# A gated-attention kernel with a fused maxout layer: the second sequence's z fetched and transposed one step earlier, and a shorter lead time for one diagonal group

## The chip, the cores and the metric

The kernel runs on one core of one Trainium2 chip. A core has a matrix engine (TensorE, PE in the profile, with its weight loads as PEld), a vector engine (VectorE, DVE), a scalar engine (ScalarE, ACT), a general engine (GpSimd, POOL) and a queueing engine (SyncE, SP). They run side by side, each in its own program order, and wait for each other by semaphores. PSUM is the memory that TensorE writes; 16 DMA engines move data between memories. The metric is the device time of one execution in microseconds (us), as the median of several runs.

## The reference

Eight sequences of 3072 rows. Each goes through an attention with squared, rectified scores, is gated by u, and the result goes through a two-branch maxout layer:

```python
scale = 1.0 / S                                          # S = 3072, D = 256, d_qk = 64
scores = scale * np.matmul(z, z.transpose(0, 2, 1))
attn = np.maximum(scores, 0.0) ** 2
x = u * np.matmul(attn, v)                               # x: 24576 x 256
h1 = x @ w1                                              # d_ff = 1024
h2 = x @ w2
out = np.maximum(h1, h2) @ w_out
```

The kernel takes max(h1, h2) as max(x (w1 - w2), 0) + h2, so that the second branch folds into one matrix W2o = w2 @ w_out.

## The kernel before, in words

**Steps.** A sequence has 24 blocks of 128 rows; a step (b, s) makes the output of four of them, so there are 6 steps for each of 8 sequences, 48 in all, numbered through from 0. In step (b, s), TensorE sums 24 blocks into two PSUM tiles, `xacc0` and `xacc1` (256 columns in two halves; one buffer each, so a step's first xacc matmul waits until the step before has been read out). DVE then multiplies by u (the tile `xT`, lines 295 to 306). Three steps later (LAG = 3) the maxout part of that step runs: matmuls into `d_ps`, evicted as `g_sb` by ACT or DVE, then matmuls into `o_ps`, evicted as `o_sb` and written out. From step 4 on, all xacc, d and o matmuls are cut into half-height (64-row) ones.

**Scores.** A pair tile (n, k0) is the two score blocks k0 and k0 + 1 of step n against its four column blocks: two matmuls into `s_ps`, then ReLU on ACT (`r_sb`, line 233) and a square on DVE (`a_sb`, line 236). The score matrix is symmetric, so a pair to the right of the diagonal is also turned by a DMA transpose on SyncE's queue (`aT`) and serves a later step; in the first sequence the first four steps compute everything up to column group 3 directly. A diagonal tile (n, None) is made by `scores_diag` (line 249): four score matmuls into two buffers, one ReLU on ACT, one on DVE, four squares on DVE into `aD`, and three turns on SyncE.

**PSUM buffers.** `s_ps`, `d_ps`, `o_ps` and `w2o_ps` share three buffers (`mm_psum`, line 71) in turn.

**The order written out by hand.** The list `work` holds TensorE's work besides the scores, with nominal lengths in ns. Every item names the tiles that it reads and a latency, and a tile's due time is the item's nominal start minus that latency (line 650). Latencies: LAT_OWN for a tile read directly, LAT_TURNED for a turned one, LAT_DIAG for a diagonal (line 536, used in `put_block`, line 549). `lay` (line 678) then goes through the tiles from the last due to the first and puts each group at the last allowed spot that is not after its due time and far enough ahead of the group behind it. In the later steps a group is one tile; in the first steps it is three (WIN = 3), and in steps 0 to 2 the allowed spots are one nominal group of 2592 ns apart. The three first groups are put down by hand at the head of the kernel (`ahead`, `squared` and `third`, lines 786 to 814); among these, `third` scores the tiles (0,8) and (0,10).

**Transfers.** `plan` (line 711) gives each load and turn a nominal time, as a step and us into it; they are issued when the order of work passes that time (lines 815 to 823). Loads go out from GpSimd's queue, each behind a `gate`: a one-column copy of the newest score or g tile (line 97), which holds the load back until that tile exists. z of a sequence is loaded by `load_z` (line 103: one DMA that casts from fp32 to bf16, and two small memsets) and transposed into `zT` by `make_zT` (line 136: two DMA transposes on SyncE's queue). The times for the second sequence's z are `z_at` and `zT_at` in line 742. w_out is loaded at step 2 + 9 us and first read by `fold_w2o` in step 3 (line 187).

**Where the second sequence comes in.** The steps of the first sequence are 0 to 5. The first group that needs the second sequence's zT is the diagonal tile (6, None), which `lay` puts into step 4, behind 16 of that step's 24 blocks.

Of the kernel before, what the change touches and what calls it, by code (L numbers as in the profile page):

```python
# [11 lines left out]
def kernel(  # L12
# [32 lines left out]
    G = 4  # L45
# [487 lines left out]


    work = []
    LAT_OWN, LAT_TURNED, LAT_DIAG = 3500, 9000, 12000

    def put(ns, shares, fn, reads=()):
        work.append((ns, shares, fn, reads))
# [9 lines left out]
    def put_block(st, k):  # L549
        row = NG * st.b + st.s  # L550
        if k // G in st.early:
            reads = [((NG * st.b + k // G, k0), LAT_TURNED) for k0 in (G * st.s, G * st.s + 2)]
            put(216, False, lambda: st.add_early(k), reads)
        elif k // G == st.s and st.diag:
            put(216, False, lambda: st.add_diag(k % G), [((row, None), LAT_DIAG)])
        else:
            put(216, False, lambda: st.add_own(k), [((row, k - k % 2), LAT_OWN)])

# [19 lines left out]
    for n, st in enumerate(steps):  # L578
# [4 lines left out]
        if st.halves:  # L583


            blocks = [G * i + j for i in st.early for j in range(G)]
            blocks += [k for k0 in own for k in (k0, k0 + 1)]
            if st.diag:
                blocks += [G * st.s + j for j in range(G)]
            put_three_d(n - LAG)  # L590
            within = dict(zip((4, 10), put_d_halves(n - LAG, 6)))
            for i, k in enumerate(blocks):
                within.get(i, lambda: None)()
                put_block(st, k)
            put_all_o(n - LAG)
            within = {}
            if n == len(steps) - 1:
                within = dict(zip((14, 20), put_d_halves(n - LAG + 1, 6)))
                within[4] = lambda: put_three_d(n - LAG + 1)
            for i in range(NSB):  # L600
                within.get(i, lambda: None)()
                put(216, False, lambda st=st, i=i: st.other_way(i))
            continue
# [107 lines left out]
    def plan(b, s, us, is_load, fn):  # L711
        transfers.append((start_of[b, s] + us * 1000, len(transfers), is_load, fn))

    def plan_load(b, s, us, fn):
        plan(b, s, us, True, fn)

    def fetch_u(b, s):
        seqs[b].u_sb[s] = load_u(b, s)

    def turn_u(b, s):  # L720
        seqs[b].uT[s] = make_uT(seqs[b].u_sb[s])

    def fetch_z(b):
        seqs[b].z_sb = load_z(b, [NSB])
        seqs[b].v = new_v()

    def turn_z(b):
        seqs[b].zT = make_zT(seqs[b].z_sb)

    def fetch_v(b, i):  # L730
        load_v(b, seqs[b].v, i * G, G)

    for n, st in enumerate(steps):
        b, s = st.b, st.s
        if n + 1 < len(steps):
            nx = steps[n + 1]
            plan_load(b, s, 5 if st.halves else 2, lambda nx=nx: fetch_u(nx.b, nx.s))
        plan(b, s, 1, False, lambda b=b, s=s: turn_u(b, s))
        if s == 0 and b + 1 < B:
            c = b + 1  # L740
            if b == 0:
                z_at, zT_at = (3, 5), (4, 4)
                v_at = [(4, 8), (4, 14), (5, 1), (5, 6), (5, 11), (5, 15)]
            else:
                z_at, zT_at = (0, 7), (3, 3)
                v_at = [(s, 14) for s in range(NG)]
            plan_load(b, *z_at, lambda c=c: fetch_z(c))
            plan(b, *zT_at, False, lambda c=c: turn_z(c))
            for i, at in enumerate(v_at):
                plan_load(b, *at, lambda c=c, i=i: fetch_v(c, i))  # L750
# [103 lines left out]
```

## Time and profile before

| | |
|---|---|
| median of 3 runs | 977.18 us (976.05 to 978.23) |
| the profiled execution's own time | 974.66 us |
| its span, first to last instruction | 972.9 us |
| mean granted TensorE clock | 0.996 of full speed |
| DVE, ACT, POOL busy | 40%, 50%, 8% |
| DMA transposes and stores (queue q1), share of the 16 DMA engines' span | 66.0% |
| DMA loads with a cast (queue q0) | 23.3% |

The page gives busy times by engine and groups of instructions. `L77` is the line of a helper that records all matmuls, so groups are told apart by their tiles: `xacc<-a_sb,v_sb` adds a block whose scores are read directly, `xacc<-aT,v_sb` one that was turned, `xacc<-aD,v_sb` a diagonal one, `s_ps<-zT` are scores. `64*128` is a half-height matmul, two of which run side by side. In a timeline row stand the start in us from the start of the span, the length, the engine, line and operation, the tiles written and read, the count, and in brackets the idle time ahead of it with what ended it. Lengths of neighbouring matmuls overlap, so a rate is read from start to start. SPq is SyncE's queue: its lengths are those of issuing, not of the transfer. A row of the windows view has the window, its length, then for PE, PEld, DVE, ACT and POOL the busy time and the count, then the granted clock, the DMA share and GB/s.

### The profile page before, as it was taken

The numbers are of one execution on the slowest core, as the hardware profiler recorded it, in microseconds if no ns is written. First come the engines' busy times: TensorE is split into PE (matmuls) and PEld (weight loads), VectorE is DVE, ScalarE is ACT, GpSimd is POOL, SyncE is SP. The second block draws the span as 40 slices with busy tenths as digits, with TensorE's granted clock in tenths as the row PEclk, the third lists the DMA queues.
The fourth block names the chain that finished last, engine by engine and source line by source line (L and its number), as shares of the span: only waits on it lengthen the run. The fifth ranks groups of instructions, "written<-read, shape, count | busy, mean of one in ns | idle before, by whom it ended". The sixth has DMA issues, their size and how long they took to land.

```text
span 972.9 us, 24379 instructions
## 1 busy us (share of the span) xinstructions
PE 956.9 (98%) x10446; PEld 590.5 (61%) x10446; DVE 391.5 (40%) x648; ACT 485.9 (50%) x533; POOL 78.9 (8%) x228
## 2 busy tenths in 40 slices
PE   8996999999999999999999999999999999999998
PEld 3353655676667666666666666666666666666666
DVE  5662344334532454325433344333444333442211
ACT  6863445445553555445554454544555545554323
POOL 2110110000000001000010001000000000000000
PEclk9998999999999999999999999999999999999999
DMA  8997999989999899997998989978899889875411
GB/s 138 152 155 141 161 157 185 156 134 174 111 178 172 129 196 131 158 184 132 168 168 141 170 147 147 194 132 153 144 155 190 152 138 168 153 139 112 102 42 66
DMA packets 378557, 144.07 MB, mean 148 GB/s; under 512 B 356945, under 2 KB 358609, under 8 KB 378449
## 3 DMA queue, kind: packets, MB, share of 16 engines
q1 hardware_dynamic: 361888, 112.78, 66.0%
q0 software_dynamic: 16560, 29.74, 23.3%
q8 instruction: 81, 1.33, 0.6%
q14 instruction: 28, 0.22, 0.1%
HBM read 59.77 MB, written 25.17 MB: 87 GB/s over the span
## 4 chain that ended last, share of the span: by engine, by line
PE 96%; DMA 2%; DVE 1%; ACT 1%; issue 0%; SPq 0%; POOL 0%; DVEq 0%; POOLq 0%
PE xacc L77 51%; PE o_ps L77 22%; PE d_ps L77 16%; PE s_ps L77 7%; DMA v_sb<-in_v_dram 1%; DMA zT<-z_sb 1%; ACT r_sb L233 0%; DMA o_sb<-in_z_dram 0%; DVE g_sb L513 0%; PE tpz L149 0%; DVE a_sb L236 0%; PE w2o_ps L77 0%; DVE r_sb L231 0%; ACT r_sb L261 0%; ACT zT L150 0%
## 5 line engine op out<-in xcount | busy, mean ns | idle before, releaser
L77 PEld LDWEIGHTS <-v_sb 64*128 64x128 bf16 (+1 forms) x4416 | 255.5, 94 | 232.9 <-issue 8.3
L233 ACT ACTIVATE r_sb<-s_ps 128x1024 bf16<-128x1024 f32 x258 | 260.7, 1024 | 161.9 <-PE s_ps L77 159.1
L236 DVE TENSOR_TENSOR a_sb<-r_sb 128x1024 bf16<-128x1024 bf16 x260 | 179.4, 691 | 398.2 <-ACT r_sb L233 395.1
L77 PE MATMUL xacc<-a_sb,v_sb 64*128 64x512 bf16 (+1 forms) x1888 | 254.0, 377 | 1.2 <-DMA v_sb<-in_v_dram 1.0
L77 PE MATMUL xacc<-aT,v_sb 64*128 64x512 bf16 x1824 | 228.8, 376 | 0.0
L77 PE MATMUL o_ps<-w_out_sb,g_sb 64*128 64x256 bf16 (+1 forms) x3008 | 202.0, 269 | 0.4 <-ACT g_sb L513 0.2
L77 PE MATMUL d_ps<-xT,w_sb 64*128 64x512 bf16 (+1 forms) x1520 | 191.1, 376 | 0.2 <-ACT g_sb L513 0.2
L513 ACT ACTIVATE g_sb<-d_ps 128x1024 bf16<-128x1024 f32 x127 | 124.8, 1021 | 107.9 <-PE d_ps L77 105.2
L77 PEld LDWEIGHTS <-g_sb 64*128 64x128 bf16 (+1 forms) x3008 | 166.6, 94 | 11.8 <-issue 1.0
L77 PEld LDWEIGHTS <-w_sb 64*128 64x128 bf16 (+1 forms) x1520 | 85.5, 94 | 77.9 <-issue 1.3
L527 ACT COPY o_sb<-o_ps 128x512 f32<-128x512 f32 x92 | 53.8, 585 | 150.8 <-PE o_ps L77 150.8
L77 PE MATMUL s_ps<-zT 64*128 64x512 bf16 (+3 forms) x696 | 117.5, 357 | 9.1 <-DMA zT<-z_sb 7.9
L77 PE MATMUL xacc<-aD,v_sb 64*128 64x512 bf16 x704 | 92.2, 378 | 0.0
L513 DVE TENSOR_SCALAR g_sb<-d_ps 128x1024 bf16<-128x1024 f32 x61 | 74.7, 1225 | 39.9 <-PE d_ps L77 31.2
L77 PE MATMUL o_ps<-W2o_sb,xT 64*128 64x256 bf16 (+1 forms) x752 | 76.0, 269 | 0.0
L263 DVE TENSOR_SCALAR r_sb<-s_ps 128x384 bf16<-128x384 f32 x44 | 24.5, 558 | 112.3 <-PE s_ps L77 112.3
L77 PEld LDWEIGHTS <-zT 64*128 64x128 bf16 x696 | 37.3, 94 | 50.3 <-issue 9.3
L299 DVE SCALAR_TENSOR_TENSOR xT<-xacc,uT 128x512 bf16<-128x512 f32 x96 | 61.9, 683 | 14.5 <-PE xacc L77 14.5
L261 ACT ACTIVATE r_sb<-s_ps 128x896 bf16<-128x896 f32 x44 | 40.3, 917 | 49.8 <-PE s_ps L77 49.1
L98 POOL COPY gate_sb<-a_sb 128x1 bf16<-128x1 bf16 x75 | 14.4, 192 | 582.5 <-DVE a_sb L236 404.4
L77 PEld LDWEIGHTS <-xT 64*128 64x128 bf16 (+1 forms) x752 | 42.2, 94 | 0.4
L101 POOL DMA_DIRECT2D u_sb<-in_u_dram x48 | 25.5, 531 | 18.3 <-issue 17.6
(40 smaller groups left out, 127.8 us busy)
## 6 DMA issues: line engine op xcount, KB each, us to landing
out_dram<-o_sb SPq DMA_DIRECT2D x47, 512.0 KB, 3.4
v_sb<-in_v_dram POOLq DMA_DIRECT2D x48, 256.0 KB, 5.4
u_sb<-in_u_dram POOLq DMA_DIRECT2D x48, 256.0 KB, 5.2
aT<-a_sb SPq DMA_TRANSPOSE x228, 4.9
z_sb<-in_z_dram POOLq DMA_DIRECT2D x7, 384.0 KB, 8.8
aD<-aD SPq DMA_TRANSPOSE x132, 3.7
w_sb<-in_moe_w_dram POOLq DMA_DIRECT2D x2, 512.0 KB, 7.7
uT<-u_sb SPq DMA_TRANSPOSE x48, 3.8
```

The source lines that it names most:

```text
L77: return pin(nc.tensor.matmul(*args, **kw))
L98: pin(nc.gpsimd.tensor_copy(gate_sb, tile_ap))
L101: pin(nc.gpsimd.dma_start(**kw))
L233: keep(nc.scalar.activation(r_sb, s_ps, AF.Relu))
L236: keep(nc.vector.tensor_mul(a_sb, r_sb, r_sb))
L261: nc.scalar.activation(r_sb, s_ps[:, 0:7, :], AF.Relu)
L263: nc.vector.tensor_single_scalar(out=r2_sb, in_=s2_ps[:, 2:5, :], scalar=0.0, op=ALU.max)
L299: nc.vector.scalar_tensor_tensor(out=xT[:, dc, :].rearrange("p (t q) -> p t q", q=P), in0=xacc[dc].rearrange("p (t q) -> p t q", q=P), sca ...
L513: nc.any.tensor_single_scalar(out=g_sb, in_=d_ps, scalar=0.0, op=ALU.max)
L527: nc.any.tensor_copy(o_sb[:, ds(t, 2), :], o_ps[:, :, :D])
```

## The change

Two edits. The diagonal tiles of the first sequence (there are two of them: steps 4 and 5) get a latency of their own, 9500 instead of 12000, so their due time is 2.5 nominal us later. The second sequence's z is loaded at step 2 + 6 us instead of step 3 + 5 us, and transposed at step 3 + 8 us instead of step 4 + 4 us.

```diff
-    LAT_OWN, LAT_TURNED, LAT_DIAG = 3500, 9000, 12000
+    LAT_OWN, LAT_TURNED, LAT_DIAG_0, LAT_DIAG = 3500, 9000, 9500, 12000
...
-            put(216, False, lambda: st.add_diag(k % G), [((row, None), LAT_DIAG)])
+            put(216, False, lambda: st.add_diag(k % G), [((row, None), LAT_DIAG if st.b else LAT_DIAG_0)])
...
             if b == 0:
-                z_at, zT_at = (3, 5), (4, 4)
+                z_at, zT_at = (2, 6), (3, 8)
                 v_at = [(4, 8), (4, 14), (5, 1), (5, 6), (5, 11), (5, 15)]
```

## The prediction

> **What bounds the kernel now.** I read the page's busy times first, then the list of waits on TensorE, then the timeline around the longest of them.
>
> ```profile
> PE 956.9 (98%) x10446; PEld 590.5 (61%) x10446; DVE 391.5 (40%) x648; ACT 485.9 (50%) x533; POOL 78.9 (8%) x228
> ...
> PE s_ps L77 <- DMA zT<-z_sb: 7.9, 1, 7.9
> ...
> PE xacc L77 <- DMA v_sb<-in_v_dram: 1.0, 1, 1.0
> ```
>
> TensorE is busy for 98% of the span, so only what makes it wait, or run slowly, can pay. One wait is far longer than the rest: once, a score matmul waits 7.9 us for the transpose of a z. The timeline of TensorE shows where, with two groups ahead of it that ran undisturbed (start, length, tiles, count, and in brackets the idle time before it):
>
> ```profile
> 78.95 1.03 PE L77 MATMUL xacc<-aT,v_sb 64*128 64x512 bf16 x8
> 79.82 0.38 PE L77 MATMUL s_ps<-zT 64*128 64x512 bf16 x2
> ...
> 82.46 1.46 PE L77 MATMUL xacc<-aT,v_sb 64*128 64x512 bf16 x12
> 91.80 0.71 PE L77 MATMUL s_ps<-zT 64*128 64x512 bf16 x4 [7.88 <-DMA zT<-z_sb]
> 92.31 1.91 PE L77 MATMUL xacc<-a_sb,v_sb 64*128 64x512 bf16 x8
> 94.02 1.54 PE L77 MATMUL xacc<-aD,v_sb 64*128 64x512 bf16 x8
> 95.40 0.38 PE L77 MATMUL s_ps<-zT 64*128 64x512 bf16 x2
> ...
> 84.00:96.00 12.00, 4.20 (x30) 1.91 (x32) 1.64 (x6) 1.16 (x3) 1.24 (x3) 0.72 0.81 126
> ```
>
> The waiting group is the four score matmuls of the second sequence's first diagonal. After it TensorE is slow as well: eight half-height xacc matmuls take 0.87 us from 78.95 to 79.82, but 1.71 and 1.38 us from 92.31 and 94.02. The row of the 12 us window gives the reason: its granted clock (the third number from the end) is 0.72 of full speed.
>
> **The z transfers.** SyncE's queue and the landing times of the two transposes:
>
> ```profile
> 83.35 3.96 SPq L92 DMA_TRANSPOSE zT<-z_sb  x2
> ...
> DMA to landing us min/median/max: 6.0/6.5/7.0
> ...
> 62.61 0.53 POOL L101 DMA_DIRECT2D z_sb<-in_z_dram  x1 [0.26 <-issue]
> ...
> 83.04 1.02 ACT L513 ACTIVATE g_sb<-d_ps 128x1024 bf16<-128x1024 f32 x1
> ```
>
> They are issued at 83.35, just as TensorE comes to need them, and the second lands some 7 us later. The change puts the z load one step earlier on GpSimd's queue (ahead of w_out and the next u) and the transposes into step 3 on SyncE's queue, behind the turn of tile (3,16) and ahead of those of (3,18) to (3,22). That place on SyncE comes at about 62 to 66 us, so they land near 72, some 12 us before their use. The gain here is 7.88 us of idle time, plus the clock: 1.71 + 1.38 - 2 x 0.87 = 1.35 for the xacc matmuls, and half of the 0.51 us (91.80 to 92.31) of the four scores, 0.25: 1.6 together. In the sum: **-9.5**. Behind the wait something new can show: the diagonal needs two score buffers, and one belongs to a d_ps whose ACT eviction ended at 84.06, while TensorE stood ready at about 83.9. I charge **+0.2** (0 to 0.5).
>
> What SyncE is moved past: its two zT issues take 3.96 us in step 3, where the three turns behind them are used only in step 4. Step 4's diagonal turns now stand ahead of its uT instead of far ahead of the step; that uT is used at the step's end. So SyncE's order costs nothing unless it runs over 10 us late there.
>
> **The start.** The new latency (9500 for 12000) moves the due time of group {(4,diagonal), (4,20)} so that it falls into a later place, near the end of step 3; the place it leaves is taken by the group before, and so on down to the front. The order of instructions shows it: six score matmuls (tiles 12, 14, 16) leave the spot ahead of the first xacc matmul, and each of the 14 groups from there to (3,22) stands one place later. TensorE, before:
>
> ```profile
> 9.21 0.61 PE L77 MATMUL xacc<-blank 128*128 128x512 bf16 x2
> 10.14 0.61 PE L77 MATMUL s_ps<-zT 64*128 64x512 bf16 x4 [0.32 <-DVE zT L150]
> 11.26 0.39 PE L77 MATMUL s_ps<-zT 64*128 64x512 bf16 x2 [0.51 <-ACT r_sb L233]
> 11.58 1.04 PE L77 MATMUL xacc<-a_sb,v_sb 128*128 128x512 bf16 x4
> 12.55 0.93 PE L77 MATMUL s_ps<-zT 64*128 64x512 bf16 x4
> 13.41 1.90 PE L77 MATMUL xacc<-a_sb,v_sb 128*128 128x512 bf16 x8
> 15.25 0.61 PE L77 MATMUL s_ps<-zT 64*128 64x512 bf16 x4
> ...
> 16.68 2.75 PE L77 MATMUL xacc<-a_sb,v_sb 128*128 128x512 bf16 x12 [0.21 <-DVE a_sb L236]
> 19.36 0.82 PE L77 MATMUL s_ps<-zT 64*128 64x512 bf16 x6
> 20.11 2.76 PE L77 MATMUL xacc<-a_sb,v_sb 128*128 128x512 bf16 x12
> ...
> 23.56 2.76 PE L77 MATMUL xacc<-a_sb,v_sb 128*128 128x512 bf16 x12
> ...
> 8.50 0.68 DVE L236 TENSOR_TENSOR a_sb<-r_sb 128x1024 bf16<-128x1024 bf16 x1
> 10.00 1.28 DVE L236 TENSOR_TENSOR a_sb<-r_sb 128x1024 bf16<-128x1024 bf16 x2
> 22.68 0.69 DVE L236 TENSOR_TENSOR a_sb<-r_sb 128x1024 bf16<-128x1024 bf16 x1 [0.22 <-ACT r_sb L233]
> ...
> 2.14 3.18 POOL L101 DMA_DIRECT2D v_sb<-in_v_dram  x6
> DMA to landing us min/median/max: 5.8/5.8/5.8
> ```
>
> The early scores wait for zT and for a score buffer, and hold up everything in order behind them. From the end of the blanks (9.82) to 19.36, 9.54 us pass. Without the six scores the same xacc work is: four matmuls 0.97 (11.58 to 12.55), four scores about 0.5 (from six in 0.75, 19.36 to 20.11), eight matmuls 1.84, six scores 0.75, twelve matmuls 2.68: 6.74 us, ending at 16.56, 2.80 earlier. Inputs are there: the first square ends at 9.18, the first v chunk lands at 2.14 + 5.8 = 7.9, the next two squares end at 11.28, when the eight matmuls start at 11.29. One group of six scores is then still owed, and is paid at the new place at the end of step 3: 0.75. Net **-2.05**; bounds 0 (another wait takes over) and -2.3.
>
> Do the later places hurt? The group scored at 19.36 has its third square done at 22.68 + 0.69 = 23.37. One place later its first tile is read at 23.56 and its third 8 matmuls after, near 25.3: 1.9 us to spare, so I cost it at nothing. The step ends need the first two tiles together, with about 1 us to spare.
>
> **The new place of the diagonal.** At the end of step 3 its evictions now meet the epilogue (xT) on DVE, and step 4's first xacc matmul waits for both xT.
>
> ```profile
> 65.71 0.56 DVE L263 TENSOR_SCALAR r_sb<-s_ps 128x384 bf16<-128x384 f32 x1 [0.89 <-PE s_ps L77]
> ...
> 67.21 0.22 DVE L267 TENSOR_TENSOR aD<-r_sb 128x128 bf16<-128x128 bf16 x1
> ...
> 76.35 2.76 PE L77 MATMUL d_ps<-xT,w_sb 64*128 64x512 bf16 x24
> ```
>
> The diagonal's five DVE instructions take 1.72 us (65.71 to 67.43), the square of (4,20) 0.69 and, in the changed order, stand partly ahead of the second xT (0.68 each, the length of the other DVE work of that size). From the start of the scores DVE needs about 0.5 + 1.72 + 0.3 for ACT + 0.69 + 2 x 0.68 = 4.6 us; TensorE meanwhile has the scores 0.75, eight matmuls 1.84 and the 24 d matmuls 2.60 (76.35 to 78.95), 5.2. So 0.6 us are left and it costs nothing; bounds 0 and +0.5. The turned diagonal is read 7 us after step 4 begins (blocks first); with its three turns issued behind the output of the first chunk it should land some 2 us before that.
>
> **The loads.** z now stands ahead of w_out, whose first reader is the w2o matmul:
>
> ```profile
> 50.75 0.69 DVE L236 TENSOR_TENSOR a_sb<-r_sb 128x1024 bf16<-128x1024 bf16 x1 [0.70 <-ACT r_sb L233]
> ...
> 55.58 0.89 POOL L101 DMA_DIRECT2D w_out_sb<-in_moe_w_out_dram  x1 [0.28 <-issue]
> ...
> 67.55 1.91 PE L77 MATMUL w2o_ps<-w_out_sb,w2T_sb 128*128 128x256 bf16 x16
> ...
> z_sb<-in_z_dram POOLq DMA_DIRECT2D x7, 384.0 KB, 8.8
> ...
> w_out_sb<-in_moe_w_out_dram POOLq DMA_DIRECT2D x1, 512.0 KB, 6.4
> ```
>
> z's gate reads the square that ends at 51.44, so with the start 2.8 us earlier it issues near 49.1; w_out near 52.8; w2o needs it at 64.75. If w_out moved nothing until z had landed, it would land at 49.1 + 8.8 + 6.4 = 64.3: just in time. I take 0; the bounds are 0 and about +4 (z as long again by half).
>
> The Trainium skill (DMA: Bandwidth & Descriptors, section "Anatomy of one DMA") fits a transfer on the gpsimd path as 2.0 us plus its bytes over 436 GB/s; by it z's 786 KB of fp32 would take an estimated 3.8 us, against 8.8 measured beside transposes, w_out would have 5 us to spare, and the sum would be the same. The same page (section "Queues, rings and completion order") has each DMA engine alternate between its queues packet by packet, which speaks against the change: z then slows the turns of step 2 instead of those of step 3. No price follows from it, as those turns are read in steps 4 and 5.
>
> The v wait of 1.0 us lies in step 6, with all its loads gated by compute; it moves along and stays (bounds -1.0 and +1).
>
> **The sum.** Against the profiled execution's own 974.66 us (a span of 972.9 and 1.8 around it): -9.5 + 0.2 - 2.05 = -11.35, so 963.3. The median of the runs shown, 977.18, lies 2.5 above that execution, and I carry this over: **965.8 us**.
>
> **The rivals.**
> - *The wait goes, the start gains nothing* (0.18): the first xacc matmuls wait for v or a square, or the step ends lose what the start brings. For it: only 0.01 us lies between the second pair of squares and its reader. Against it: the waits named above are the scores' own. 977.18 - 9.3 = 967.9.
> - *A late load takes the wait's place* (0.12): w_out lands after 64.75. For it: the serial bound leaves 0.4 us. Against it: the two loads overlap. A stall of 2 to 4 us, so 968 to 970.
> - *The shorter distance makes the kernel slower* (0.05): in the 14 groups each tile is read one place, 3.45 us (20.11 to 23.56), after its scores' place instead of two. If relu and square needed 1.9 us more than they show, TensorE would wait in every group; to eat the 11.35 us it must lose 11.35 / 14 = 0.8 us in each, that is tiles 2.7 us later than the trace has them; at 3 us later, 14 x 1.1 = 15.4 against 11.35, so 977.18 + 4 = 981. For it: ACT is busy nearly without a break there. Against it: the 1.9 us.
> - *The change doesn't remove the wait* (0.03): zT still lands too late, or the diagonal of step 4 waits as long. For it: SyncE blocks in order. Against it: 12 us of room. Near 977, less what the start gives, 975 to 977.
>
> **How the numbers follow.** The forecast has 0.62. Its own range is 963.5 to 967; with the first two rivals, and a wait that may have been longer in the executions without a profile, 962.5 to 970.0 leaves out the last two and a little at the low end. A measurement of this kernel tells 0.2% (2 us) from no change. Faster by more: 0.62 + 0.18 + 0.12, 0.92; slower, 0.05; within, 0.03.
>
> **What would show it.** Right: no TensorE wait on zT; the granted clock at 1.00 in all windows from 72 to 96; zT issued near 62 to 66; the first xacc matmul on v near 9.9 and the twelfth group's end (now 19.36) near 16.6; step 4's first d group some 2 us earlier, the second sequence's first scores 10 us earlier. Wrong: xacc matmuls in steps 0 to 3 with idle time on DVE, w2o waiting for w_out, the aD blocks waiting for their turns, or a v wait in step 6 that has grown by what was won.

## The result and the profile after

| | before | after |
|---|---|---|
| median of the runs taken side by side | 977.5 us (4 runs, 976.05 to 978.23) | 961.53 us (4 runs, 960.77 to 962.40) |
| the profiled execution's own time | 974.66 us | 962.40 us |
| its span | 972.9 us | 960.6 us |
| mean granted TensorE clock | 0.996 | 0.999 |

The ratio of after to before is 0.9839 (95% interval 0.9822 to 0.9856): 16.0 us faster. The forecast was 965.8 us, so the kernel came out 4.3 us faster than that, and 1 us below the lower end of the range. Between the two profiled executions the difference is smaller, 974.66 - 962.40 = 12.26 us, against 11.35 forecast.

The page's busy times and the list of waits on TensorE, after (total, times, longest, in us):

```profile
PE 952.8 (99%) x10439; PEld 585.1 (61%) x10446; DVE 391.6 (41%) x648; ACT 486.0 (51%) x533; POOL 79.9 (8%) x228
...
PE xacc L77 <- DVE blank L400: 1.2, 1, 1.2
PE xacc L77 <- DMA v_sb<-in_v_dram: 0.9, 1, 0.9
PE tpz L149 <- DMA z_sb<-in_z_dram: 0.7, 1, 0.7
```

The wait on zT has gone. Of the three longest that are left, two lie at the very start; the wait on v is the one of step 6. (The clock of 0.999 is that of the whole span; it is below 1.00 only in about the last microsecond.) TensorE's timeline around the place of the old wait, after:

```profile
79.99 1.46 PE L77 MATMUL xacc<-aT,v_sb 64*128 64x512 bf16 x12
81.28 0.43 PE L77 MATMUL s_ps<-zT 64*128 64x512 bf16 x4
81.56 1.03 PE L77 MATMUL xacc<-a_sb,v_sb 64*128 64x512 bf16 x8
82.42 1.03 PE L77 MATMUL xacc<-aD,v_sb 64*128 64x512 bf16 x8
83.28 0.38 PE L77 MATMUL s_ps<-zT 64*128 64x512 bf16 x2
```

The twelve matmuls that began at 82.46 begin at 79.99 now, the 2.47 us that the start has won. The scores follow at once, where 7.9 us stood empty, and the two groups of eight take 0.86 us each from start to start instead of 1.71 and 1.38. The windows view says the same of the clock (third number from the end), in two windows of the kernel after:

```profile
72.00:84.00 12.00, 12.00 (x112) 5.69 (x112) 8.70 (x20) 7.72 (x9) 1.24 (x4) 1.00 0.77 139
84.00:100.00 16.00, 16.00 (x188) 8.99 (x186) 5.94 (x9) 8.42 (x10) 1.62 (x5) 1.00 0.97 166
```

What made this possible stands on the queues. SyncE's issue of the two zT transposes with their landing times, and GpSimd's issues of z and of w_out, after:

```profile
59.56 4.37 SPq L92 DMA_TRANSPOSE zT<-z_sb  x2
DMA to landing us min/median/max: 4.7/5.1/5.5
...
48.96 0.53 POOL L101 DMA_DIRECT2D z_sb<-in_z_dram  x1
52.12 0.89 POOL L101 DMA_DIRECT2D w_out_sb<-in_moe_w_out_dram  x1 [0.28 <-issue]
```

The transposes end on the queue at 63.9 and have landed by 69.5 at the latest, some 12 us ahead of 81.28. The start of the kernel after, TensorE:

```profile
8.95 0.60 PE L77 MATMUL xacc<-blank 128*128 128x512 bf16 x2
9.39 0.81 PE L77 MATMUL xacc<-a_sb,v_sb 128*128 128x512 bf16 x3
10.35 0.60 PE L77 MATMUL s_ps<-zT 64*128 64x512 bf16 x4
10.89 1.90 PE L77 MATMUL xacc<-a_sb,v_sb 128*128 128x512 bf16 x8
12.72 0.82 PE L77 MATMUL s_ps<-zT 64*128 64x512 bf16 x6
13.48 2.76 PE L77 MATMUL xacc<-a_sb,v_sb 128*128 128x512 bf16 x12
16.17 0.82 PE L77 MATMUL s_ps<-zT 64*128 64x512 bf16 x6
```

The first groups don't keep their places: the first xacc matmuls on v stand ahead of any score now and find their tiles ready, and the twelve matmuls that ended at 19.36 end at 16.17. The scores left out are paid at the end of step 3, where the diagonal now stands, with DVE's last row of that step below TensorE's:

```profile
71.45 0.66 PE L77 MATMUL s_ps<-zT 64*128 64x512 bf16 x6
72.05 1.90 PE L77 MATMUL xacc<-a_sb,v_sb 128*128 128x512 bf16 x8
73.88 2.76 PE L77 MATMUL d_ps<-xT,w_sb 64*128 64x512 bf16 x24
76.48 1.03 PE L77 MATMUL xacc<-aT,v_sb 64*128 64x512 bf16 x8
...
74.78 0.68 DVE L299 SCALAR_TENSOR_TENSOR xT<-xacc,uT 128x512 bf16<-128x512 f32 x1
```

The second xT ends at 75.46, 1.0 us ahead of the first xacc matmul of step 4. Paired matmul by matmul, by their starts, the two traces differ by -2.47 us at the end of step 3 (0.26 of it because the blanks end earlier), by -12.12 behind the old wait, and by a constant -12.24 from 137 us to the end: all of the change lies in the first 140 us.

What is left there is the wait on v, in step 6 (timeline, after):

```profile
122.11 1.04 PE L77 MATMUL xacc<-a_sb,v_sb 64*128 64x512 bf16 x8 [0.95 <-DMA v_sb<-in_v_dram]
```

### The profile page after: what moved, and what is told of

Same layout as the page of the kernel before. It is cut to its first block, busy times and chain, and to the rows that moved or that the text cites. A ratio compares the mean times of both kernels' runs of the same rounds, so it can differ in the third digit from the quotient of the medians.

```text
span 960.6 us, 24374 instructions
## 1 busy us (share of the span) xinstructions
PE 952.8 (99%) x10439; PEld 585.1 (61%) x10446; DVE 391.6 (41%) x648; ACT 486.0 (51%) x533; POOL 79.9 (8%) x228
## 4 chain that ended last, share of the span: by engine, by line
PE 97%; DMA 2%; DVE 0%; issue 0%; ACT 0%; POOL 0%; POOLq 0%; DVEq 0%
PE xacc L77 51%; PE o_ps L77 22%; PE d_ps L77 17%; PE s_ps L77 7%; DMA v_sb<-in_v_dram 1%; DMA z_sb<-in_z_dram 1%; DVE g_sb L513 0%; PE w2o_ps L77 0%; PE tpz L149 0%; ACT r_sb L233 0%; DVE a_sb L236 0%; ACT o_sb L527 0%; DVE o_sb L348 0%; POOL ident masks.py:199 0%; POOL gate_sb L98 0%
## 5 line engine op out<-in xcount | busy, mean ns | idle before, releaser
L77 PEld LDWEIGHTS <-v_sb 64*128 64x128 bf16 (+1 forms) x4416 | 252.5, 94 | 234.5 <-issue 6.6
L513 DVE TENSOR_SCALAR g_sb<-d_ps 128x1024 bf16<-128x1024 f32 x61 | 74.7, 1225 | 39.0 <-PE d_ps L77 30.4
```

Of the source, the lines that this page charges most:

```text
L77: return pin(nc.tensor.matmul(*args, **kw))
L513: nc.any.tensor_single_scalar(out=g_sb, in_=d_ps, scalar=0.0, op=ALU.max)
```

## The experiments

Two accounts of the missing 4.3 us stood against each other. By the first, it belongs to the wait: the two profiled executions are no typical pair, and what varies between executions of the kernel before is what the move of z takes away. By the second, it is a gain that the forecast put too low somewhere else: the start, the distance between scores and their readers, or the length of an execution as such. Each part was done alone, the kernels before and after were profiled again, and single waits were taken out or filled. Diffs are against the kernel named.

**The move of z alone** (against before):

```diff
-                z_at, zT_at = (3, 5), (4, 4)
+                z_at, zT_at = (2, 6), (3, 8)
```

> Only the z load and its transposes move; the latency of the diagonals stays at 12000. Between the profiled executions of before and after, 9.65 us went at the wait on zT and 2.5 at the start. But the medians lie 16.0 apart. Theory A (the wait on zT differs in length from execution to execution, and the profiled one of before was short): this kernel gains 12 to 14 us in the median, more than the 9.65 of the trace, and its executions lie within 1.5 us of each other. Theory B (the waits at the start vary): 9.7 us in the median, and the spread stays at 2 us or more. Theory C (the profiled execution of before was short all over): 9.7 us, and the latency alone 2.5, with some 4 us that belong to neither.

Measured: 963.68 us (4 runs, 962.79 to 964.73), ratio 0.9873 (0.9859 to 0.9888): -12.4 us, where the forecast's terms for this part were -9.3. Its runs lie within 1.9 us of each other (1.5 were expected). TensorE has no wait on zT; its longest wait is a new one behind uT's transpose, whose landing times follow (timeline, and landing of uT's transposes between 90 and 160 us, of this kernel):

```profile
139.06 1.04 PE L77 MATMUL xacc<-aT,v_sb 64*128 64x512 bf16 x8 [1.51 <-DVE xT L299]
...
DMA to landing us min/median/max: 4.2/7.3/12.6
```

So the larger part of what the forecast lacked comes with z, and 1.5 us of what z brings is given back in step 6.

**The shorter latency alone** (against after):

```diff
-                z_at, zT_at = (2, 6), (3, 8)
+                z_at, zT_at = (3, 5), (4, 4)
```

> Only the latency of the first sequence's diagonals goes from 12000 to 9500; z is loaded and transposed at the old times. By the prediction the start gains 2.05 us (2.5 by the trace of after), and the wait on zT stays, since SyncE's queue reaches zT as much earlier as TensorE does. Theory A: 2 to 3 us faster in the median, spread over 2 us as before, and a TensorE wait on zT of 7 us or more in the profile. Theory B: 5 to 6 us faster. A third possibility, that TensorE arrives earlier but zT doesn't: 0 to 1 us faster, with a wait of some 10 us.

Measured: 973.01 us (8 runs, 970.43 to 975.55), ratio 0.9967 (0.995 to 0.9984): -3.2 us, within its interval the 2.05 of the forecast. Its profiled execution took 974.75 us and shows why a single one says little (timeline):

```profile
88.76 0.72 PE L77 MATMUL s_ps<-zT 64*128 64x512 bf16 x4 [7.23 <-DMA zT<-z_sb]
...
132.89 1.89 PE L77 MATMUL xacc<-a_sb,v_sb 64*128 64x512 bf16 x8 [2.87 <-DMA v_sb<-in_v_dram]
```

The wait on zT starts earlier by what the start wins, and the wait on v was 2.87 us in this execution; the eight matmuls behind it ran at half rate (1.89 us). That gave back all that the start had won. The two parts make -12.4 - 3.2 = -15.6, and the whole was measured as -14.8 and -16.0 us, so within these runs neither takes from the other.

**The kernel before, profiled three more times** (no edit):

> The kernel before, unchanged, for a second profile and more times. Theory A: its wait on zT differs from 7.9 us by the same amount as its own time differs from 974.66. Theory B: the wait is 7.9 and the first group of twelve xacc matmuls (16.68 in the first profile) starts that much later. Theory C: the difference is spread over the span.

> The kernel before, a third profile. If the length of the early waits sets an execution's time, then own time, wait on zT and wait on v go together: 974.66 us with 7.9 and 1.0, 976.01 with 8.4 and 1.0; an execution of 978 us should show some 2 us more of these two waits together, with the clock's loss, and none elsewhere. If the difference lies elsewhere, the two waits stay at 8.9 to 9.4 whatever the time.

> The kernel before, a fourth profile. If the half-rate stretch is 6.8 us, the execution takes 974 to 975.5 us; if it is 10.2, 975.5 to 977.5; a longer time than that shows a second stretch behind the wait on v.

Measured: 975.54 us (12 runs), 976.40 us (12 runs), and 977.99 us in a single one. The windows view of the first, profiled before the forecast, and then of the second and of the fourth:

```profile
84.00:100.00 16.00, 8.20 (x104) 5.38 (x106) 2.33 (x7) 2.59 (x4) 1.24 (x3) 0.79 0.81 129
130.00:144.00 14.00, 12.99 (x162) 7.86 (x160) 4.59 (x6) 5.88 (x8) 1.84 (x7) 1.00 1.14 147
```

```profile
84.00:100.00 16.00, 8.05 (x78) 4.68 (x80) 2.33 (x6) 1.94 (x2) 1.11 (x3) 0.68 0.76 117
```

```profile
130.00:144.00 14.00, 11.58 (x132) 6.86 (x130) 3.90 (x5) 4.43 (x5) 1.68 (x6) 0.88 1.20 148
```

Matmuls behind the wait took twice their time, so a slow stretch is one at half rate, and its length is twice the missing clock times the window: (1 - 0.79) x 16 x 2 = 6.7 us in the first (6.8 in narrower windows, where the rounding of the clock counts for less), (1 - 0.68) x 16 x 2 = 10.2 in the second, (1 - 0.88) x 14 x 2 = 3.4 at v in the fourth. The waits of the second and of the fourth (timelines):

```profile
91.95 0.71 PE L77 MATMUL s_ps<-zT 64*128 64x512 bf16 x4 [8.41 <-DMA zT<-z_sb]
```

```profile
92.19 0.72 PE L77 MATMUL s_ps<-zT 64*128 64x512 bf16 x4 [8.23 <-DMA zT<-z_sb]
136.02 1.79 PE L77 MATMUL xacc<-a_sb,v_sb 64*128 64x512 bf16 x8 [2.42 <-DMA v_sb<-in_v_dram]
```

| profile of the kernel before | own time | wait on zT | half rate around it | wait on v | half rate at v |
|---|---|---|---|---|---|
| first (the one shown before) | 974.66 | 7.88 | 6.8 | 1.0 | none |
| third | 975.00 | 7.85 | 6.8 | 1.4 | none |
| second | 976.01 | 8.41 | 10.2 | 1.0 | none |
| fourth | 977.99 | 8.23 | 6.8 | 2.4 | 3.4 |

The four differ in these columns and hardly anywhere else. Against the first, the second falls back by 1.79 us around the wait on zT (0.53 of wait, the rest of clock) and stays at +1.40 from 99 us to the end; the fourth falls back by 3.1 us at v and stays at +3.36 from 137 us on. The first had the short form of every one of them: it was the best of the four.

The mean granted clock of the 84 later executions of the kernel before (three of them the profiled ones) points the same way:

| mean granted clock | executions | mean time, us | from, to |
|---|---|---|---|
| 0.996 | 25 | 974.65 | 972.24, 975.74 |
| 0.995 | 43 | 976.56 | 973.67, 978.81 |
| 0.994 | 11 | 976.83 | 976.05, 978.36 |
| 0.993 | 4 | 979.22 | 978.07, 980.63 |
| 0.991 | 1 | 982.37 | |

Their median is 976.03 and they spread over 10 us. The clock doesn't sort them fully: 0.994 lies only 0.3 us above 0.995, and within 0.995 they differ by 5 us. Eight executions of the kernel after have a clock of 0.999 or 1.000, a median of 961.4 and a spread of 2.2 us (960.36 to 962.54).

**The earlier transposes with the load left late** (against before):

```diff
-                z_at, zT_at = (3, 5), (4, 4)
+                z_at, zT_at = (3, 5), (3, 8)
```

> z is loaded at the old time (step 3 + 5 us) and only its transposes are moved to step 3 + 8 us; the latency stays at 12000. They then stand in SyncE's queue ahead of the turns of (3,18) to (3,22) and wait there for z, which landed at about 71 us in the trace of before. If the place of the transposes in SyncE's queue made the wait, this kernel gains as much as the one with both z moves, within 1 us; the turns behind are issued after 71 us and still come in time. If the late load made it, it gains less than half.

**The earlier load with the transposes left late** (against before):

```diff
-                z_at, zT_at = (3, 5), (4, 4)
+                z_at, zT_at = (2, 6), (4, 4)
```

> The other half of the z moves: the load at step 2 + 6 us, the transposes at the old place (step 4 + 4 us), latency 12000. If SyncE's order alone set the wait, nothing is gained: a wait on zT of 7 to 9 us stays, the median within 1.5 us of before. If the late load set it, most of the 12.5 us is gained.

Measured: the transposes alone 966.84 us (7 runs, from 963.59 to 976.61), ratio 0.9884 (0.9866 to 0.9903; by the medians -9.4 us); the load alone 975.66 us (12 runs), ratio 0.9995 (0.9982 to 1.0007), with a wait on zT as long as ever (timeline of the kernel with the earlier load):

```profile
91.37 0.72 PE L77 MATMUL s_ps<-zT 64*128 64x512 bf16 x4 [7.75 <-DMA zT<-z_sb]
```

So the place of the transposes in SyncE's order makes the wait, not the load. But with the load left late the executions differ by 13 us: three of the seven, at 963.6 to 964.0, are as fast as with both moves, and four are 3 to 13 us slower. The profiled one was the slowest (SyncE's queue, then TensorE, of the kernel with the earlier transposes):

```profile
62.15 12.93 SPq L92 DMA_TRANSPOSE aT<-a_sb  x3
75.36 3.43 SPq L92 DMA_TRANSPOSE zT<-z_sb  x2
133.92 5.89 SPq L92 DMA_TRANSPOSE uT<-u_sb  x1
...
148.05 1.89 PE L77 MATMUL xacc<-aT,v_sb 64*128 64x512 bf16 x8 [7.99 <-DVE xT L299]
```

zT is issued at 75.36 instead of 59.56, after three turns that took 12.93 us; that is still early enough, and TensorE was 9.5 us ahead at 99 us. Then it stood 8 us for an xT, which had no uT yet: uT's transpose was issued at 133.92 to 139.81 and took up to 12.7 us to land. In the profile of the kernel with both moves of z the same transpose was issued at 125.04. So the late load made SyncE late, by some 9 us at that point, and TensorE paid for it in step 6; that the other slow executions have the same reason is not shown.

**The kernel after once more** (no edit), **and with v loaded a place earlier** (against after):

```diff
-                v_at = [(4, 8), (4, 14), (5, 1), (5, 6), (5, 11), (5, 15)]
+                v_at = [(3, 14), (4, 8), (4, 14), (5, 1), (5, 6), (5, 11)]
```

> The changed kernel, unchanged, on the same chip as the others. The runs so far gave 12.5 us for the z moves alone and 3.2 for the latency alone, against a before of 976.2 us on this chip. If the two add up, this kernel is 14.5 to 16 us faster and lies 2 to 3 us below the z moves alone (963.7). If the latency is worth less once the wait is gone, it lies within 1 us of 963.7. If the first 160 us hold all that differs between executions, its trace keeps a constant distance to the first trace of the changed kernel from there on.

> The changed kernel with each of the second sequence's six v loads one place earlier (from step 3 + 14 us to step 5 + 11 us), so that the last one doesn't land after its reader. If the load's time is all that makes the 0.95 us wait on v, this wait goes and the kernel is about 1 us faster than the changed one, with a smaller spread. If the loads then slow SyncE's turns earlier instead, xT waits for uT, or the blocks of step 4 wait for their turns, and it is as fast or slower.

Measured: 961.22 us (4 runs), ratio 0.9845 (0.9826 to 0.9864), and with the earlier v 961.44 us (5 runs, 961.11 to 961.53), ratio 0.9845 (0.9827 to 0.9863). The second profile of the kernel after took 962.54 us and has no wait on v; it has another one (timeline, and w_out's landing):

```profile
65.67 1.91 PE L77 MATMUL w2o_ps<-w_out_sb,w2T_sb 128*128 128x256 bf16 x16 [0.81 <-DMA w_out_sb<-in_moe_w_out_dram]
...
DMA to landing us min/median/max: 13.1/13.1/13.1
```

w_out was 0.8 us late in this execution, after 13.1 us on its way. The earlier v takes its own wait out of the profile (own time 961.27), yet the median doesn't move by what the runs can tell. The second profile also shows that the early place isn't fixed: its zT was issued at 68.06 instead of 59.56, behind four turns and a uT that took SyncE 11.1 and 6.8 us, and landed at 74.7, still 8 us ahead of its use at 82.57.

**The wait filled with work** (against before): 32 matmuls of the zero tile into a buffer of their own, put just ahead of the scores that wait. The results are unused; the wait on zT stays, but TensorE is busy for most of it. The extra tile also takes one turn of the three PSUM buffers.

```diff
+        if (6, None) in windows[w]:
+            fill = mm_psum.tile([P, 2, GW], fp32, name="fill", tag="mm")
+            for i in range(32):
+                matmul(fill[:, i % 2, :], blank[:, :P], blank, start=True, stop=True)
```

> The kernel before, with 32 matmuls of a zero tile (6.9 us) put ahead of the four score matmuls that wait for zT; they write a score buffer that nobody reads, so that TensorE is busy while it would wait. The traces of before show the half-rate stretch of the clock as 6.8 us long in two (974.7 and 975.0 us) and as 10.2 in one (976.0). If the clock's stretch is a cost of its own that differs from execution to execution, the granted clock stays at 1.00 here, the wait shrinks to some 1 us, the kernel is 1.6 to 3 us faster than before in the median and its executions lie closer together. If the wait alone differs, it gains 1.6 at most and the spread stays. If the clock costs nothing, the time is that of before.

Measured: 971.9 us (12 runs, 970.57 to 979.68), ratio 0.9971 (0.9951 to 0.999): -2.8 us, by its interval between -1 and -4.8, with TensorE kept busy in most of the wait. The medians lie further apart, by 4.5 us, as three executions of 975.56 us and more hold the ratio up. Against what was expected, the executions don't lie closer together (9.1 us, against 6.6 in the kernel before). The clock was 1.000 in 8 of the 12; one of these took 975.56 us all the same, so not all that varies is clock. The profiled one was the slowest of the twelve (timeline):

```profile
82.99 7.08 PE L77 MATMUL fill<-blank 128*128 128x512 bf16 x32
92.23 0.45 PE L77 MATMUL s_ps<-zT 64*128 64x512 bf16 x4 [2.16 <-DMA zT<-z_sb]
...
93.38 1.82 PE L77 MATMUL xacc<-aD,v_sb 64*128 64x512 bf16 x8
...
137.64 1.73 PE L77 MATMUL xacc<-a_sb,v_sb 64*128 64x512 bf16 x8 [3.79 <-DMA v_sb<-in_v_dram]
```

The filling covered all but 2.16 us of the wait. In this execution the clock still fell twice, a microsecond after the filled wait (1.82 us for eight matmuls) and behind the wait on v (1.73 us), which is the longest seen, 3.79 us. So the filling keeps the clock up in most executions, not in all, and 2.8 us (4.5 by the medians) is a rough measure of the clock's share of the wait, against the 1.6 that the forecast read from one profile; the interval holds all three. The wait on v varies by itself, with the filling too.

**z behind w_out, v earlier** (against after):

```diff
-                z_at, zT_at = (2, 6), (3, 8)
-                v_at = [(4, 8), (4, 14), (5, 1), (5, 6), (5, 11), (5, 15)]
+                z_at, zT_at = (2, 9.5), (3, 8)
+                v_at = [(3, 14), (4, 8), (4, 14), (5, 1), (5, 6), (5, 11)]
```

> The changed kernel with the v loads one place earlier, as in the run before, and z's load behind that of w_out instead of ahead of it. The two traces of the changed kernel showed 0.95 us of waiting for v in one and 0.81 for w_out in the other. If these are all that is left, no wait over 0.3 us on a DMA is left after the start, and the median is 0.5 to 1 us below the changed one (961.2). If z now lands too late for its transposes, SyncE's queue stands still in step 3 and a wait on xT, aD or zT comes up; then it is 1 us or more slower.

Measured: 961.11 us (5 runs, 960.88 to 961.95), ratio 0.9847 (0.9829 to 0.9865). Its profiled execution (960.88 us) has no wait on a load left. It is the lowest median of all, but it lies only 0.1 us below the second median of the kernel after, not the 0.5 to 1 us expected, and that is less than these runs can tell.

## Why the forecast was right in its steps and wrong in its number

**The wait on zT: right, its clock too small.** zT is issued at 59.56 to 63.93, forecast "about 62 to 66" (at 68.06 to 72.32 in the second profile), and the clock is 1.00 in every window there. The term was -9.5. Between the two profiles the place gave 12.12 - 2.47 = 9.65, so it fitted that pair; but the 1.6 of clock was the short form. With 10.2 us at half rate it costs more: the second profile lost 1.26 us more to the clock, so about 2.9.

**The PSUM buffer: not there.** The +0.2 didn't show: with zT in time the four scores follow the twelve matmuls without a gap (79.99, 81.28, 81.56).

**The start: right.** -2.05 forecast, -2.47 in the trace, or -2.21 without the 0.26 by which the blanks ended earlier; the shorter latency alone gave -3.2, and against the move of z alone the whole change gives 963.68 - 961.22 = 2.5. The rival in which the start gains nothing is out, and so is the shorter distance that slows every group: no xacc matmul of steps 0 to 3 waits for DVE behind the blanks.

**The diagonal's place: right.** It was costed at nothing with 0.6 us to spare; the second xT ended 1.0 us early.

**The loads: right, and close.** The serial bound had w_out land 0.4 us before its use. In the first profile it came in time; in the second it was 0.8 us late. So the late load is real in some executions, at a fifth to two fifths of the price that its rival named (2 to 4 us).

**The wait on v: right for the pair.** It "moves along and stays": 1.0 and 0.95 us. What the forecast didn't see is that it varies (1.0 to 2.4 us in the four profiles of the kernel before, 3.8 in the filled one, none in the second profile of the kernel after), and in its long form takes 3.4 us at half rate with it.

**The step that failed** is the last one: "The median of the runs shown, 977.18, lies 2.5 above that execution, and I carry this over". Carrying it over takes what sets an ordinary execution of the kernel before apart from the profiled one for a constant that the change doesn't touch. The profiles and the clocks show the reverse. An ordinary execution is longer because its wait on zT, the stretch at half rate around it or the wait on v is longer, and the change takes the first two away. The range did name "a wait that may have been longer in the executions without a profile", but lowered its end by 1 us for it (963.5 to 962.5), where the median of the 84 executions lies 1.4 us above the profiled one. In numbers: 4.3 us lie between 965.8 and 961.53. Of these, 2.52 are the offset that was carried over; 12.26 - 11.35 = 0.91 are the terms of the sum, put too low; and 962.40 - 961.53 = 0.87 because the profiled execution after is one of the long ones of its kernel. From the profile's own time the terms alone gave 963.3, 1.8 above the result. Part of the 2.52 is chance: over 84 executions the median before is 976.03, so the three runs shown lay 1.1 us above it; the other 1.4 us are the profiled execution's luck, as its waits and its half-rate stretch were short. Against 976.03, the eight executions of the kernel after (median 961.4) gain 14.6 us.

**What stays open.** Why v lands later in some executions was not settled. Its last load was issued at 123.35, 123.62 and 123.87 us in the first profile, the fourth and the filled one, and took 11.0, 12.4 and 13.7 us to land: what differs is the time on the way, not the issue. That the wait on v stays short in the kernel after rests on two profiles and on a spread of 2.2 us over eight executions. And the rows by clock suggest that time goes with half-rate stretches, but not at which place each of the 84 had them; the places are known for the four that were profiled.

## What to carry to other kernels

Where a change removes a wait, ask of the difference between the profiled execution and the median what it is made of before it is carried over: if it is the wait that varies, it goes with the wait. Several profiles of the same kernel tell this for little; the mean clock of every run gives a hint. And a tile that comes too late has two places, that of its load and that of its transpose: here the place in the transposing queue set the wait, and the load's place set how steady the gain was.

## What the runs showed of the hardware that was not expected

**The clock is lost in whole steps.** All stretches at half rate behind a wait were 3.4, 6.8 or 10.2 us long, one, two or three times the same step. A wait of 7.88 us had two steps and one of 8.41 us three. The length of the wait doesn't decide: the fourth profile's 8.23 us had two, and the 7.75 us of the kernel with the earlier load had three (granted clock 0.50 from 86.94 to 97.18). What goes with the count is how far the wait reaches into the second step of the stretch: by 0.1 to 0.7 us in the four profiles with two steps (the first, the third, the fourth, and the shorter latency alone), by 1.0 to 1.2 us in the three with three (the second, the earlier load, and the earlier transposes, whose wait is that on xT). No experiment varied this alone, so it is a pattern and not a shown cause. A step in which TensorE is busy throughout costs half its length, 1.7 us, and the groups of 84 executions at 0.996 and 0.995 lie 1.9 us apart. The Trainium skill (TensorE: Matmul & The Clock Gate, section "Part 1: The HAM clock gate (the "warmup" mystery)") has the clock follow a free-running window of about 3.4 us and warns that the number of slow matmuls at a kernel's start varies from run to run for that reason; the traces agree on the window, with 3.4, 6.8 and 10.2, in the middle of a kernel.

**A short wait can be enough.** 2.42 us on v in the fourth profile of the kernel before brought a step of 3.4 us, and so, by the 1.82 us of eight matmuls, did the 2.16 us left in the filled kernel; 1.43 us on v in the third profile brought none.

**Transposes are slow to issue beside a load.** At the same place of step 3, three turns of score tiles took SyncE 12.93 us (4.3 us each) in the kernel with only the transposes moved, whose z load was issued at 62.81, right beside them, and 4.15 us (1.4 each) in the kernel with both moves of z, whose z had landed at 57.9. The two kernels differ in the load's place alone. The other such pair agrees: 10.82 us in the kernel before, 4.58 in the kernel with the earlier load. These lengths hold some waiting for the tiles that are turned. GpSimd's row of the late load, and SyncE's row of the turns with both moves:

```profile
62.81 0.53 POOL L101 DMA_DIRECT2D z_sb<-in_z_dram  x1 [0.26 <-issue]
```

```profile
63.71 4.15 SPq L92 DMA_TRANSPOSE aT<-a_sb  x3
```
